# Transposing the query in four pieces, and giving the last unit's products banks of their own with its pieces added and stored one by one

## Chip, cores, metric

One core of one Trainium2 chip. The metric is the device time of one execution, in microseconds (us), as the median of several executions. A ratio in this text is the mean time of one kernel's fast runs over the mean of the other's fast runs of the same rounds, so it is not quite the ratio of the medians that are quoted beside it.

## The reference

```python
def _attn_ref(q, k, v, g_norm):                  # 8 batches x 8 heads x 576 tokens x 64
    kv = np.einsum('bhsd,bhse->bhde', k, v)
    out = np.einsum('bhsd,bhde->bhse', q, kv)
    rms = np.sqrt(np.mean(out * out, axis=-1, keepdims=True) + 1e-06)
    return out / rms * g_norm

def _moe_ref(x, w_a, w_b, w_out):                # 4608 tokens, 512 -> 1536 -> 512
    return (x @ w_a) * (x @ w_b) @ w_out
```

The second takes the first's output, tokens by (heads x 64), as x.

## The kernel before

The program is recorded as nodes (engine, estimated duration, priority, dependencies with latencies, buffers) and put in order by a greedy planner while the kernel is built. **The planner's durations and latencies set only the order of the instructions on each engine; on the chip each instruction waits for semaphores.** An estimate that is too short can therefore not give a wrong result.

```python
class Plan:
    LAT = {"PE": 0.27, "SP": 2.2, "ACT": 0.2, "DVE": 0.18}
    # ... ready(): end of each dependency plus LAT, or plus the latency given with it
    # ... order(): per engine, what can start first; then the lower priority

def load_node(b, prio, dep, xt=None):            # loads of one batch; cut
    def issue():                                 # on GpSimd
        if dep is not None:                      # wait for the q of the batch before
            nc.gpsimd.tensor_copy(gate_t, dep["q"].tile[0:1, 0, 0:1])
        # ... q to DRAM as bf16 (2 DMAs, scr), then k (5 DMAs) and v (2 DMAs) into SBUF
    def transpose():                             # on SP
        nc.sync.dma_start_transpose(
            out=ld["q"].tile[:].rearrange("p a s -> p (a s)"),
            in_=scr[:].rearrange("a s h d -> (a s) (h d)"))
    ld["n"]  = plan.add("POOL", issue_us, prio, issue, [(dep["qn"], 8.0)] ...)
    ld["qn"] = plan.add("SP", 2.5, prio, transpose, [(ld["n"], q_us)], [ld["q"]])

def load_wo(dep):                                # output weights, behind the first such q
    def issue():
        nc.gpsimd.tensor_copy(gate_t, dep["q"].tile[0:1, 0, 0:1])
        # ... two DMAs, wo_t
    return plan.add("POOL", 1.8, 50.0, issue, [(dep["qn"], 8.0)])
```

The output product of the first 512 tokens (`o_std`) has matmuls of 128x512. Its nodes depend on `(wo_n, 5.8)` for the first half and `(wo_n, 10.6)` for the second.

The later output products use seven block products in place of eight (a Winograd form of Strassen's scheme). The last unit, whose stores end the kernel:

```python
# m = 2 row tiles of 128 rows, EH = 256 columns; X, Y, Z, W[i] are PSUM banks
p1 = prod(0, X, a11, b11, True, [], [X])
e1 = ev(0, 0, 0, p1, [ob])                                       # ACT copies X
p2 = prod(1, Y, a12, b21, True, [], [Y])
c11 = comb(1, 0, 0, Y, [p2, e1], [Y])                            # DVE adds
p6 = prod(2, X, sx(s2), t2, False, [e1, n2], (), [s2], 2)        # adds into X
e2 = ev(2, 0, 1, p6)
p5 = prod(3, Z, a21, t1, True, [n1], [Z], (), 1)
e5 = ...                                                         # ACT copies Z to u5
p7 = prod(4, X, sx(s3), t3, False, [e2, n3], (), [s3], 0)        # adds into X
e3 = ev(4, 1, 0, p7)                                             # ACT copies X
c22 = comb(4, 1, 1, X, [p7, e5], [X, u5], u=u5)                  # DVE reads X
p3 = prod(5, Z, sx(s4), b22, False, [e5, n4], (), [s4], 3)       # adds into Z
c12 = comb(5, 0, 1, Z, [p3, e2], [Z])
# ... stores of c11, c22, c12
for i in range(m):
    p4 = prod(6 + 0.1 * i, W[i], a22, t4, True, [n4], [W[i]], subs=slice(i, i + 1))
    c21 = comb(6 + 0.1 * i, 1, 0, W[i], [p4, e3], [W[i]], slice(i, i + 1))
    # ... store of this piece
```

Of the kernel before, what the change touches and what calls it, by code (L numbers as in the profile page):

```python
# [137 lines left out]
def kernel(  # L138
# [11 lines left out]
    nc = tc.nc  # L150
# [258 lines left out]
    def act_us(n, bias=False):  # L409
        return (0.155 if bias else 0.06) + n / 1200  # L410
# [10 lines left out]
        ]  # L421

    T0 = 20.0
    B5, B6, CX, CY = 5, 8, 3, 4
    TB, TURN, AHEAD = 5, 3.0, 8.0
    plan = Plan({"PE": 5.7, "DVE": 3.3, "ACT": 2.7, "SP": 5.0, "POOL": 22.5, "V": 0.0})
# [180 lines left out]
    def late_batch(b, load, win):  # L607
        at = Attn(b)
        w0, w1 = win
        kb, vb, qb = load["k"], load["v"], load["q"]  # L610
        kd = Buf(RKD)
        at.qt = [qb, kd]

        def view(t):
            return t[:, 0 : H * (NCH + 1) * D].rearrange("p (h c d) -> p h c d", h=H, d=D)

        s = Buf(RS5 if b >= TB else RS)

        def kv_mm():
            kv_ps = s.tile[:].rearrange("p (a e) -> p a e", a=NP)  # L620
            for c in range(NCH + 1):
                for p in range(NP):
                    hs = slice(2 * p, 2 * p + 2)
                    nc.tensor.matmul(  # L624
                        kv_ps[:, p, :],
                        lhsT=kb.tile[:, c, hs, :],
                        rhs=view(vb.tile)[:, hs, c, :],
                        start=(c == 0 and p == 0),
                        stop=(c == NCH and p == NP - 1),
                    )  # L630

        n = plan.add(
            "PE", 1.15, w0, kv_mm, [(load["n"], load["kv_us"]), plan.at(w0 - 3)], [s, kd], [kb, vb]
        )

        def kv_out():
            kv_ps = s.tile[:].rearrange("p (a e) -> p a e", a=NP)
            at.kvd = kd.tile
            nc.scalar.copy(at.kvd[0:D, :, 0:D], kv_ps[0:D, :, 0:D])
            nc.scalar.copy(at.kvd[D:, :, D:], kv_ps[D:, :, D:])  # L640
            for p in range(NP):
                at.q[p] = qb.tile[:, p, :]

        m = plan.add("ACT", 0.75, w0, kv_out, [n], (), [s])
        if b >= TB:
            return token_tiles(at, (w0 + 0.12 * (w1 - w0), w1), [m, (load["qn"], 8.0)])
        slices(at, (w0 + 0.12 * (w1 - w0), w1), lambda p: [m, (load["qn"], 8.0)])


    def load_node(b, prio, dep, xt=None):  # L650
        ld = {"k": Buf(RK), "v": Buf(RV), "q": Buf(RQT)}
        scr = scr_pool.tile([NP, S, 2, D], BF16, name="scr", tag="scr")

        def issue():
            if dep is not None:
                nc.gpsimd.tensor_copy(gate_t, dep["q"].tile[0:1, 0, 0:1])
            if xt is not None:
                nc.gpsimd.tensor_copy(gate_t, xcols(NP - 1, (b - 2) * S, 1)[0:1])
            qv = q[b].rearrange("(p hl) s d -> hl s p d", hl=2)
            for hl in range(2):  # L660
                nc.gpsimd.dma_start(  # L661
                    out=scr[:, :, hl, :].rearrange("p s d -> s p d"), in_=qv[hl]
                )
            kt = ld["k"].tile
            ks = k[b, :, 0:SA, :].rearrange("h (sp c) d -> sp h c d", c=NCH)
            for c in range(NCH):
                nc.gpsimd.dma_start(out=kt[:, c], in_=ks[:, :, c, :])  # L667
            nc.gpsimd.dma_start(out=kt[0:SB, NCH], in_=k[b, :, SA:S, :].rearrange("h sp d -> sp h d"))
            for n, src in (("v", v),):
                t = ld[n].tile[:, 0 : H * (NCH + 1) * D].rearrange(  # L670
                    "p (h c d) -> p h c d", h=H, d=D
                )
                nc.gpsimd.dma_start(
                    out=t[:, :, 0:NCH, :],
                    in_=src[b, :, 0:SA, :].rearrange("h (sp c) d -> sp h c d", c=NCH),
                )
                nc.gpsimd.dma_start(
                    out=t[0:SB, :, NCH, :], in_=src[b, :, SA:S, :].rearrange("h sp d -> sp h d")
                )

        def transpose():
            nc.sync.dma_start_transpose(
                out=ld["q"].tile[:].rearrange("p a s -> p (a s)"),
                in_=scr[:].rearrange("a s h d -> (a s) (h d)"),
            )

        issue_us, q_us, ld["kv_us"] = (15.4, 4.3, 13.0) if dep is None else (9.0, 5.0 if b == 3 else 1.8, 16.0 if b == 3 else 13.0)

        ld["n"] = plan.add(
            "POOL", issue_us, prio, issue, ([(dep["qn"], 8.0)] if dep else []) + ([(xt, TURN)] if xt else []), [ld["k"], ld["v"]]  # L690
        )
        ld["qn"] = plan.add(
            "SP", 2.5, prio, transpose, [(ld["n"], q_us)], [ld["q"]]
        )
        return ld

# [1 line left out]

    def load_wo(dep):
        def issue():  # L700
            nc.gpsimd.tensor_copy(gate_t, dep["q"].tile[0:1, 0, 0:1])
            for i in range(2):
                sl = slice(i * FC // 2, (i + 1) * FC // 2)
                nc.gpsimd.dma_start(out=wo_t[:, sl, :], in_=wo_v[:, sl, :])

        return plan.add("POOL", 1.8, 50.0, issue, [(dep["qn"], 8.0)])


    def std_block(win):
# [257 lines left out]
    def o_unit(r0, ab, muls, osum, pr, du, chunks, pieces, m, w, first, second, X, Y, Z, ob, s2, s3, s4, W):  # L967
# [6 lines left out]
        def sx(b):  # L974
            return lambda js: b.tile[:, js, 0:w]
# [52 lines left out]
        def bank(b, subs):  # L1028
            n = subs.stop - subs.start
            return b.tile[:, subs.start * EH : subs.stop * EH].rearrange("p (s e) -> p s e", s=n)  # L1030
# [6 lines left out]
        def ev(off, fi, h, dep, takes=(), frees=()):  # L1037
            return plan.add(
                "ACT", act_us(m * EH), pr + off * du,
                lambda: nc.scalar.copy(o(fi, h), bank(X, every)), [dep], takes, frees,  # L1040
            )

        def comb(off, fi, h, ps, deps, frees=(), subs=every, u=None):
            def add():
                other = u.tile[:, subs] if u else o(fi, h, subs)
                nc.vector.tensor_add(o(fi, h, subs), bank(ps, subs), other)  # L1046

            return plan.add(
                "DVE", dve_us((subs.stop - subs.start) * EH), pr + off * du, add, deps, (), frees
            )  # L1050

        def put(fi, subs, deps, us=0.45, queue="SP", es=slice(0, d_model)):
            q = {"SP": nc.sync, "ACT": nc.scalar}[queue]

            def go():
                for i in range(subs.start, subs.stop):
                    store(r0 + (fi * m + i) * 128, ob.tile[:, fi * m + i], q, es)

            plan.add(queue, us * (subs.stop - subs.start), pr + 7 * du, go, deps, (), [ob])
# [3 lines left out]
        t2, t3, t4 = (so_t[:, i] for i in range(3))  # L1063
        n1, n2, n3, n4 = osum
        if W:
            u5 = Buf(RU)
            p1 = prod(0, X, a11, b11, True, [], [X])
            e1 = ev(0, 0, 0, p1, [ob])
            p2 = prod(1, Y, a12, b21, True, [], [Y])
            c11 = comb(1, 0, 0, Y, [p2, e1], [Y])  # L1070
            p6 = prod(2, X, sx(s2), t2, False, [e1, n2], (), [s2], 2)
            e2 = ev(2, 0, 1, p6)
            p5 = prod(3, Z, a21, t1, True, [n1], [Z], (), 1)
            e5 = plan.add(
                "ACT", act_us(m * EH), pr + 3 * du,
                lambda: nc.scalar.copy(u5.tile[:, every], bank(Z, every)), [p5], [u5],
            )
            p7 = prod(4, X, sx(s3), t3, False, [e2, n3], (), [s3], 0)
            e3 = ev(4, 1, 0, p7)
            c22 = comb(4, 1, 1, X, [p7, e5], [X, u5], u=u5)  # L1080
            p3 = prod(5, Z, sx(s4), b22, False, [e5, n4], (), [s4], 3)
            c12 = comb(5, 0, 1, Z, [p3, e2], [Z])
            e1s, e2s = slice(0, EH), slice(EH, d_model)
            put(0, every, [c11], es=e1s)
            put(1, every, [c22], es=e2s)
            for i in range(m):
                put(0, slice(i, i + 1), [c12], queue=("SP", "ACT")[i], es=e2s)
            for i in range(m):
                subs = slice(i, i + 1)
                p4 = prod(6 + 0.1 * i, W[i], a22, t4, True, [n4], [W[i]], subs=subs)  # L1090
                c21 = comb(6 + 0.1 * i, 1, 0, W[i], [p4, e3], [W[i]], subs)
                put(1, subs, [c21], queue=("ACT", "SP")[i], es=e1s)
            return
        p1 = prod(0, X, a11, b11, True, [(wo_n, 10.6)], [X])
        e1 = ev(0, 0, 0, p1, [ob])
# [45 lines left out]
    for bi in range(1, nb + 1):  # L1141
# [10 lines left out]
        ab, muls = wino_block(bi, (st[bi], st[bi + 1]), wsum)  # L1152
    o_block(
        nb, ab, muls, osum, (st[nb + 1], st[nb + 1] + o_us[nb]), NJ // 2,
        (RO, RY, RY, RS, RQ), NJ // 2,
    )
    order, t = plan.order(), 5.7
    for n in order:
# [34 lines left out]
```

## Time and profile before

| | before |
|---|---|
| time, median (range), 3 runs | 297.67 us (296.86 to 298.25) |
| span of the profiled execution | 294.8 us |
| PE busy | 288.1 us, 98% |
| end of the last matmul | 289.77 us |
| from there to the end of the span ("drain") | 5.00 us |

PE is the tensor engine, DVE the vector engine, ACT the scalar engine, POOL is GpSimd and SP only issues transfers. The trace of each kernel is of one execution, so the single times below (last matmul, drain) are those of one execution. PSUM and SBUF are the two memories on the chip in which the program's tiles lie: X, Y, Z, W and V are in banks of PSUM, inputs, weights and finished sums in SBUF. A line such as "L1008 PE MATMUL bk<-wo_t,abt" gives source line, engine, operation, and output and inputs by the program's names; in brackets stands the idle time of the engine just before and what ended it.

### The profile page before, as it was taken

How to read it: one execution, taken by the hardware profiler on the slowest of the kernel's cores; microseconds unless marked ns; L12 is line 12 of the kernel's file. 1: busy time of each engine (PE TensorE's matmuls, PEld its weight loads, DVE VectorE, ACT ScalarE, POOL GpSimd, SP SyncE). 2: the span in 40 equal slices, each digit the busy share in tenths (PEclk: the TensorE clock that was granted, in tenths of full speed). 3: DMA queues.
4: the chain of work that ended last, by engine and by line, in shares of the span. 5: the costliest groups of instructions: out<-in, count | busy, mean ns of one | idle time of the engine just before them, and what ended most of it. 6: DMA issues, size and time to landing. Idle time of an engine off the chain costs nothing.

```text
span 294.8 us, 6757 instructions
## 1 busy us (share of the span) xinstructions
PE 288.1 (98%) x2646; PEld 238.1 (81%) x2648; DVE 240.2 (81%) x441; ACT 191.7 (65%) x395; POOL 77.1 (26%) x96
## 2 busy tenths in 40 slices
PE   8999999999999999999999999999999999999993
PEld 3645558965888988899988998898988888888882
DVE  5454879893987988789979999979989958788852
ACT  3757667876578677877757866786769546665420
POOL 8945830950092470380001910000000000000000
PEclk9999999999999999999999999999999999999999
DMA  8999999699999999499816999330155001200053
GB/s 181 198 199 200 196 158 166 102 168 183 189 128 171 143 170 173 48 136 210 174 31 149 145 166 167 80 145 21 38 85 165 2 0 43 102 2 0 9 172 107
DMA packets 112643, 36.26 MB, mean 123 GB/s; under 512 B 89060, under 2 KB 108516, under 8 KB 112612
## 3 DMA queue, kind: packets, MB, share of 16 engines
q0 software_dynamic: 77552, 18.44, 65.9%
q1 hardware_dynamic: 34448, 16.70, 26.8%
q10 hardware_dynamic: 612, 0.71, 0.8%
q8 instruction: 20, 0.33, 0.5%
q14 instruction: 11, 0.09, 0.1%
HBM read 37.75 MB, written 14.75 MB: 178 GB/s over the span
## 4 chain that ended last, share of the span: by engine, by line
PE 93%; DVE 4%; issue 1%; ACT 1%; DVEq 0%; ACTq 0%
PE bk L839 47%; PE bk L1008 24%; PE bk L387 7%; PE bk L310 3%; PE bk L943 3%; PE bk L624 2%; PE bk L353 2%; PE bk L367 2%; PE bk L341 1%; PE bk L539 1%; PE bk L325 1%; DVE c L858 1%; DVE so L746 1%; DVE o_sb L1046 1%; DVE T L806 1%
## 5 line engine op out<-in xcount | busy, mean ns | idle before, releaser
L858 DVE TENSOR_TENSOR c<-bk,u 128x512 f16<-128x512 f32 x144 | 96.1, 684 | 19.3 <-PE bk L839 11.8
L420 ACT COPY u<-bk 128x512 f32<-128x512 f32 x144 | 81.4, 591 | 36.5 <-PE bk L839 29.9
L839 PE MATMUL bk<-xp,wa_t 128*128 128x256 f16 x288 | 55.0, 273 | 0.1
L839 PE MATMUL bk<-xp,wb_t 128*128 128x256 f16 x288 | 55.0, 273 | 0.0
L839 PEld LDWEIGHTS <-wa_t 128*128 128x128 f16 x384 | 37.1, 98 | 5.7 <-issue 0.3
L1008 PEld LDWEIGHTS <-abt 128*128 128x128 f16 x384 | 37.5, 98 | 4.7 <-issue 0.3
L839 PEld LDWEIGHTS <-wb_t 128*128 128x128 f16 x384 | 37.6, 98 | 4.4
L1008 PE MATMUL bk<-wo_t,abt 128*128 128x256 f16 x288 | 37.2, 273 | 0.1
L839 PE MATMUL bk<-T,sb 128*128 128x256 f16 x192 | 36.7, 273 | 0.0
L839 PE MATMUL bk<-T,sa 128*128 128x256 f16 x192 | 36.7, 272 | 0.0
L420 ACT CAST c<-bk 128x512 f16<-128x512 f32 x48 | 28.0, 587 | 12.1 <-PE bk L839 11.5
L893 DVE TENSOR_TENSOR abt<-c 128x1024 f16<-128x1024 f16 x48 | 32.7, 684 | 0.9
L839 PEld LDWEIGHTS <-sb 128*128 128x128 f16 x288 | 28.2, 98 | 3.3
L839 PEld LDWEIGHTS <-sa 128*128 128x128 f16 x288 | 27.9, 98 | 3.5
L1008 PEld LDWEIGHTS <-as 128*128 128x128 f16 x288 | 28.1, 98 | 3.3
L1040 ACT COPY o_sb<-bk 128x512 f32<-128x512 f32 x31 | 18.2, 586 | 18.5 <-PE bk L1008 18.0
L376 DVE SCALAR_TENSOR_TENSOR xp<-bk,g_col,rs 128x288 f16<-128x288 f32 x40 | 20.2, 512 | 10.9 <-ACT rs L371 10.9
L1008 PE MATMUL bk<-so,as 128*128 128x256 f16 x192 | 25.2, 273 | 0.0
L371 ACT ACTIVATE rs<-bk,eps_t 128x288 f32<-128x288 f32 x40 | 20.0, 506 | 6.2 <-PE bk L367 6.1
L667 POOL DMA_DIRECT2D k_t<-in_k_dram x24 | 21.2, 899 | 0.8 <-issue 0.5
L661 POOL DMA_DIRECT2D scr<-in_q_dram x12 | 19.6, 1638 | 2.5 <-issue 1.5
L1046 DVE TENSOR_TENSOR o_sb<-bk,o_sb 128x512 f32<-128x512 f32 (+1 forms) x25 | 16.4, 663 | 3.0 <-PE bk L1008 2.3
(107 smaller groups left out, 428.8 us busy)
## 6 DMA issues: line engine op xcount, KB each, us to landing
out_dram<-o_sb SPq DMA_DIRECT2D x20, 256.0 KB, 2.7
scr<-in_q_dram POOLq DMA_DIRECT2D x12, 288.0 KB, 8.0
k_t<-in_k_dram POOLq DMA_DIRECT2D x24, 128.0 KB, 8.2
v_t<-in_v_dram POOLq DMA_DIRECT2D x6, 512.0 KB, 11.0
out_dram<-o_sb SPq DMA_DIRECT2D x18, 128.0 KB, 2.4
wa_t<-in_moe_w_a_dram POOLq DMA_DIRECT2D x6, 256.0 KB, 10.6
wb_t<-in_moe_w_b_dram POOLq DMA_DIRECT2D x6, 256.0 KB, 10.8
wo_t<-in_moe_w_out_dram POOLq DMA_DIRECT2D x2, 768.0 KB, 9.7
```

The source lines that it names most:

```text
L371: nc.scalar.activation(rs, self.s_ps[p, h][:, 0:HF], AF.Abs_reciprocal_sqrt, bias=eps_t)
L376: nc.vector.scalar_tensor_tensor(out=xcols(p, self.b * S + h * HF, HF), in0=self.x_ps[p, h][:, 0:HF], scalar=g_col, in1=self.rs[p, h], op0 ...
L387: nc.tensor.matmul(ps[:, 0:n], lhsT=w[:, kc, fc * 128 : (fc + 1) * 128], rhs=xcols(kc, 0, n), start=(kc == 0), stop=(kc == KC - 1),)
L420: ("ACT", act_us(n), lambda: nc.scalar.copy(*args())),
L661: nc.gpsimd.dma_start(out=scr[:, :, hl, :].rearrange("p s d -> s p d"), in_=qv[hl])
L667: nc.gpsimd.dma_start(out=kt[:, c], in_=ks[:, :, c, :])
L839: nc.tensor.matmul(ps.tile[:, i * n : (i + 1) * n], lhsT=lhs(w, sm)[:, kc, :], rhs=rhs()[:, kc, :], start=start and i == 0 and kc == 0, st ...
L858: lambda: nc.vector.tensor_add(cs(fi, h), full(ps), u.tile),
L893: nc.vector.tensor_mul(t, c[:, :, :, 0], c[:, :, :, 1])
L1008: nc.tensor.matmul(ps.tile[:, sub * EH : (sub + 1) * EH], lhsT=lhs(slice(j, j + 1))[:, 0, sub * 128 : (sub + 1) * 128], rhs=rhs[:, j, :], ...
L1040: lambda: nc.scalar.copy(o(fi, h), bank(X, every)), [dep], takes, frees,
L1046: nc.vector.tensor_add(o(fi, h, subs), bank(ps, subs), other)
```

## The change

Intent: (1) q is transposed in four pieces, one per pair of heads, and the planner is told that SP is held 5.0 instead of 2.5 us, and that q is there 2.5 instead of 8.0 us after that; GpSimd's gates (one-element copies that wait for q) read the last piece. (2) In the last unit, product 7 gets a bank of its own (V) and goes ahead of product 5; products 5 and 3 go by row tile into two banks; ACT's copy of product 7 goes away; c12 is added and stored in two pieces, the last of them alone at the end.

```diff
-            return token_tiles(at, (...), [m, (load["qn"], 8.0)])
+            return token_tiles(at, (...), [m, (load["qn"], 2.5)])
 ...                                                  # the same for slices()
-                nc.gpsimd.tensor_copy(gate_t, dep["q"].tile[0:1, 0, 0:1])
+                nc.gpsimd.tensor_copy(gate_t, dep["q"].tile[0:1, NP - 1, 0:1])
 ...                                                  # the same in load_wo
-            nc.sync.dma_start_transpose(
-                out=ld["q"].tile[:].rearrange("p a s -> p (a s)"),
-                in_=scr[:].rearrange("a s h d -> (a s) (h d)"),
-            )
+            for p in range(NP):
+                nc.sync.dma_start_transpose(
+                    out=ld["q"].tile[:, p, :], in_=scr[p].rearrange("s h d -> s (h d)")
+                )
 ...
-            "POOL", issue_us, prio, issue, ([(dep["qn"], 8.0)] if dep else []) ...
+            "POOL", issue_us, prio, issue, ([(dep["qn"], 2.5)] if dep else []) ...
-            "SP", 2.5, prio, transpose, [(ld["n"], q_us)], [ld["q"]]
+            "SP", 5.0, prio, transpose, [(ld["n"], q_us)], [ld["q"]]
 ...                                                  # load_wo
-        return plan.add("POOL", 1.8, 50.0, issue, [(dep["qn"], 8.0)])
+        return plan.add("POOL", 1.8, 50.0, issue, [(dep["qn"], 2.5)])
 ...                                                  # last unit
-            e2 = ev(2, 0, 1, p6)
-            p5 = prod(3, Z, a21, t1, True, [n1], [Z], (), 1)
-            e5 = ...
-            p7 = prod(4, X, sx(s3), t3, False, [e2, n3], (), [s3], 0)
-            e3 = ev(4, 1, 0, p7)
-            c22 = comb(4, 1, 1, X, [p7, e5], [X, u5], u=u5)
-            p3 = prod(5, Z, sx(s4), b22, False, [e5, n4], (), [s4], 3)
-            c12 = comb(5, 0, 1, Z, [p3, e2], [Z])
+            e2 = ev(2, 0, 1, p6, (), [X])
+            p7 = prod(P7_AT, V, sx(s3), t3, True, [n3], [V], [s3], 0)      # P7_AT = 2.5
+            c2x = ... nc.vector.tensor_add(o(1, 0), bank(V, every), o(0, 1)) ...
+            for i in range(m):
+                p5 = prod(3 + 0.1 * i, Z[i], a21, t1, ..., subs=rows[i])
+                e5.append(... nc.scalar.copy(u5.tile[:, rows[i]], bank(Z[i], rows[i])) ...)
+            c22 = ... nc.vector.tensor_add(o(1, 1), o(1, 0), u5.tile[:, every]) ...
 ...                                                  # p4, c21 by row tile, as before
+            for i in range(m):
+                p3 = prod(6 + 0.1 * i, Z[i], sx(s4), b22, ..., subs=rows[i])
+                c12 = comb(6 + 0.1 * i, 0, 1, Z[i], [p3, e2], [Z[i]], rows[i])
+                put(0, rows[i], [c12], queue=("ACT", "SP")[i], es=e2s)
 ...
-        (RO, RY, RY, RS, RQ), NJ // 2,
+        (RO, RY, RS, RY, RS, RQ, RY), NJ // 2,
```

More of the change, by code (lines that the diff above doesn't have):

```diff
@@ L423 @@
     T0 = 20.0
+    P7_AT = 2.5
     B5, B6, CX, CY = 5, 8, 3, 4
@@ L645, in late_batch @@
         if b >= TB:
-            return token_tiles(at, (w0 + 0.12 * (w1 - w0), w1), [m, (load["qn"], 8.0)])
-        slices(at, (w0 + 0.12 * (w1 - w0), w1), lambda p: [m, (load["qn"], 8.0)])
+            return token_tiles(at, (w0 + 0.12 * (w1 - w0), w1), [m, (load["qn"], 2.5)])
+        slices(at, (w0 + 0.12 * (w1 - w0), w1), lambda p: [m, (load["qn"], 2.5)])
     def load_node(b, prio, dep, xt=None):
@@ L681, in transpose @@
         def transpose():
-            nc.sync.dma_start_transpose(
-                out=ld["q"].tile[:].rearrange("p a s -> p (a s)"),
-                in_=scr[:].rearrange("a s h d -> (a s) (h d)"),
-            )
+            for p in range(NP):
+                nc.sync.dma_start_transpose(
+                    out=ld["q"].tile[:, p, :], in_=scr[p].rearrange("s h d -> s (h d)")
+                )
         issue_us, q_us, ld["kv_us"] = (15.4, 4.3, 13.0) if dep is None else (9.0, 5.0 if b == 3 else 1.8, 16.0 if b == 3 else 13.0)
         ld["n"] = plan.add(
-            "POOL", issue_us, prio, issue, ([(dep["qn"], 8.0)] if dep else []) + ([(xt, TURN)] if xt else []), [ld["k"], ld["v"]]
+            "POOL", issue_us, prio, issue, ([(dep["qn"], 2.5)] if dep else []) + ([(xt, TURN)] if xt else []), [ld["k"], ld["v"]]
         )
         ld["qn"] = plan.add(
-            "SP", 2.5, prio, transpose, [(ld["n"], q_us)], [ld["q"]]
+            "SP", 5.0, prio, transpose, [(ld["n"], q_us)], [ld["q"]]
         )
@@ L700, in issue @@
         def issue():
-            nc.gpsimd.tensor_copy(gate_t, dep["q"].tile[0:1, 0, 0:1])
+            nc.gpsimd.tensor_copy(gate_t, dep["q"].tile[0:1, NP - 1, 0:1])
             for i in range(2):
@@ L1065, in o_unit @@
         if W:
-            u5 = Buf(RU)
+            u5, V, Z = Buf(RU), W[0], [Z, W[1]]
+            W = W[2:]
+            rows = [slice(i, i + 1) for i in range(m)]
             p1 = prod(0, X, a11, b11, True, [], [X])
@@ L1071, in o_unit @@
             p6 = prod(2, X, sx(s2), t2, False, [e1, n2], (), [s2], 2)
-            e2 = ev(2, 0, 1, p6)
-            p5 = prod(3, Z, a21, t1, True, [n1], [Z], (), 1)
-            e5 = plan.add(
-                "ACT", act_us(m * EH), pr + 3 * du,
-                lambda: nc.scalar.copy(u5.tile[:, every], bank(Z, every)), [p5], [u5],
-            )
-            p7 = prod(4, X, sx(s3), t3, False, [e2, n3], (), [s3], 0)
-            e3 = ev(4, 1, 0, p7)
-            c22 = comb(4, 1, 1, X, [p7, e5], [X, u5], u=u5)
-            p3 = prod(5, Z, sx(s4), b22, False, [e5, n4], (), [s4], 3)
-            c12 = comb(5, 0, 1, Z, [p3, e2], [Z])
+            e2 = ev(2, 0, 1, p6, (), [X])
+            p7 = prod(P7_AT, V, sx(s3), t3, True, [n3], [V], [s3], 0)
+            c2x = plan.add(
+                "DVE", dve_us(m * EH), pr + 4 * du,
+                lambda: nc.vector.tensor_add(o(1, 0), bank(V, every), o(0, 1)), [p7, e2], (), [V],
+            )
+            e5 = []
+            for i in range(m):
+                p5 = prod(3 + 0.1 * i, Z[i], a21, t1, True, [n1], [Z[i]], (), 1, subs=rows[i])
+                e5.append(
+                    plan.add(
+                        "ACT", act_us(EH), pr + 3 * du,
+                        lambda i=i: nc.scalar.copy(u5.tile[:, rows[i]], bank(Z[i], rows[i])),
+                        [p5], [] if i else [u5],
+                    )
+                )
+            c22 = plan.add(
+                "DVE", dve_us(m * EH), pr + 4.2 * du,
+                lambda: nc.vector.tensor_add(o(1, 1), o(1, 0), u5.tile[:, every]), [c2x] + e5, (), [u5],
+            )
             e1s, e2s = slice(0, EH), slice(EH, d_model)
@@ L1086, in o_unit @@
             for i in range(m):
-                put(0, slice(i, i + 1), [c12], queue=("SP", "ACT")[i], es=e2s)
+                p4 = prod(5 + 0.1 * i, W[i], a22, t4, True, [n4], [W[i]], subs=rows[i])
+                c21 = comb(5 + 0.1 * i, 1, 0, W[i], [p4, c22], [W[i]], rows[i])
+                put(1, rows[i], [c21], queue=("ACT", "SP")[i], es=e1s)
             for i in range(m):
-                subs = slice(i, i + 1)
-                p4 = prod(6 + 0.1 * i, W[i], a22, t4, True, [n4], [W[i]], subs=subs)
-                c21 = comb(6 + 0.1 * i, 1, 0, W[i], [p4, e3], [W[i]], subs)
-                put(1, subs, [c21], queue=("ACT", "SP")[i], es=e1s)
+                p3 = prod(6 + 0.1 * i, Z[i], sx(s4), b22, False, [e5[i], n4], (), [s4], 3, subs=rows[i])
+                c12 = comb(6 + 0.1 * i, 0, 1, Z[i], [p3, e2], [Z[i]], rows[i])
+                put(0, rows[i], [c12], queue=("ACT", "SP")[i], es=e2s)
             return
```

## The prediction

> **What bounds the kernel now.** I read the page's busy times and slices first, then the waits of the tensor engine, the busy times by stretch, and at the end the timeline and transfers of the last 7 us.
>
> The page of the kernel before, busy times, slices, chain:
>
> ```profile
> span 294.8 us, 6757 instructions
> PE 288.1 (98%) x2646; PEld 238.1 (81%) x2648; DVE 240.2 (81%) x441; ACT 191.7 (65%) x395; POOL 77.1 (26%) x96
> ...
> PE   8999999999999999999999999999999999999993
> ...
> PE 93%; DVE 4%; issue 1%; ACT 1%; DVEq 0%; ACTq 0%
> ```
>
> Only the first and the last slice of PE are not full, and the chain that ended last is 93% PE. PE's own waits over the whole span are two, both in the first microseconds:
>
> ```profile
> PE bk L310 <- DVE eps_t L274: 1.2, 1, 1.2
> PE bk L310 <- issue: 0.2, 1, 0.2
> ```
>
> Since "busy" is modelled from overlapping matmuls, I also went through the spacing of the matmul starts. A 256-column matmul follows the one before by 0.109 us; after 43 us only three intervals are longer than the work explains, by some 0.27 us near 80.7, 0.07 near 193.0 and 0.27 near 226.3, and none has a data wait beside it (0.6 us in all). So from 24 us to the last matmul PE is limited by its own work. By stretch (us; PE, PEld, DVE, ACT, POOL busy with counts; clock; DMA; GB/s):
>
> ```profile
> 268.00:280.40 12.40, 12.40 (x116) 11.13 (x114) 10.82 (x21) 5.08 (x9) 0.00 (x0) 1.00 0.05 17
> 280.40:289.80 9.40, 9.37 (x86) 8.15 (x84) 5.02 (x10) 2.34 (x4) 0.00 (x0) 1.00 0.38 120
> 289.80:294.80 5.00, 0.00 (x0) 0.00 (x0) 1.26 (x4) 0.00 (x0) 0.00 (x0) 0.86 0.48 157
> ```
>
> The last unit's 84 matmuls (7 products x 12) fill 280.4 to 289.8. Then 5.0 us follow without a matmul: this drain is the only place after the start where time is not PE work. Its timeline (start, length, engine):
>
> ```profile
> 288.29 1.47 PE L1008 MATMUL bk<-wo_t,as 128*128 128x256 f16 x12
> 288.49 0.59 ACT L1040 COPY o_sb<-bk 128x512 f32<-128x512 f32 x1 [1.16 <-PE bk L1008]
> 289.11 0.69 DVE L1046 TENSOR_TENSOR o_sb<-bk,u 128x512 f32<-128x512 f32 x1 [3.80 <-ACT o_sb L1040]
> 289.72 1.34 DVE L1046 TENSOR_TENSOR o_sb<-bk,o_sb 128x256 f32<-128x256 f32 x3
> 289.83 1.80 SPq L911 DMA_DIRECT2D out_dram<-o_sb  x4
> 290.21 1.29 ACTq L911 DMA_DIRECT2D out_dram<-o_sb  x2
> ```
>
> Product 7 ends at 288.45. ACT copies the shared bank X until 289.08, and only then may DVE begin c22 from the same bank; the two halves of c21 follow, and c12, whose matmuls ended at 289.77 (0.27 after the last start, 289.50), comes last, 290.38 to 291.06 (the third of the group at 289.72). So DVE starts c12 0.6 us late and does it in one 512-column piece. All six stores are issued between 289.83 and 291.24, and their data run back to back (stretch 288 to 295 in 40 slices of 0.175 us):
>
> ```profile
> DMA  0000000000000006979999999999800000000000
> GB/s 0 0 0 0 0 0 0 0 0 0 0 0 0 0 0 217 328 240 339 345 345 334 322 369 328 334 351 339 281 24 0 0 0 0 0 0 0 0 0 0
> ```
>
> Six stores of 128 KB are 0.79 MB; at some 335 GB/s that is 2.35 us, which is what the full slices show (290.6 to 293.2). SP sees the last landing at 293.55; checks and barriers take to 294.76.
>
> **What the Trainium skill says.** "PSUM — Partial Sum Buffer", section "PSUM bank collisions raise a hardware error": two engines may not touch one bank and quadrant at the same time, two readers included, so ACT and DVE reads of one bank have to be ordered. The trace agrees: c22 starts 0.03 us after the ACT copy of the same bank. "VectorE: DVE Perf Modes", "The perf-mode tier table": a float32 tensor_tensor runs at 1x whether it reads SBUF or PSUM. That matters for the new c22, which reads SBUF alone; no such operation is in this trace, so I take the 0.69 us of the PSUM one. "DMA: Bandwidth & Descriptors", "Anatomy of one DMA": a transfer has a fixed cost of about 2.0 us, mostly the receipt of the last byte. The lone store at 285.34 landed after 1.7 us, the six of the end after 2.0 to 2.3, so the trace agrees roughly, and shows that queueing adds 0.3 to 0.6.
>
> **The change part by part.**
>
> First part, the q pieces. One DMA transpose of all of q becomes four, one per head pair. Existing rows give both forms: the whole one (qT), and pieces of the same size in another place (xp), with SP's own time for one instruction (min/median/max ns) and time to landing:
>
> ```profile
> L682 SPq DMA_TRANSPOSE qT<-scr x6: 5981/6398/6860, 42.0 to 171.8; - x6
> L594 SPq DMA_TRANSPOSE xp<-xs x12: 1152/1254/2024, 153.4 to 219.4; - x12
> ...
> qT<-scr SPq DMA_TRANSPOSE x6, 10.3
> xp<-xs SPq DMA_TRANSPOSE x12, 2.7
> ```
>
> Before: q is there 10.3 us after the issue. After: the fourth piece is issued 3 x 1.30 = 3.9 us after the first (their starts lie 1.3 apart) and lands 2.7 later, 6.6 us in all; SP is held 5.2 instead of 6.4 us. So q is ready some 3.7 us earlier, six times, and the next load can follow earlier. Who waits for q:
>
> ```profile
> POOL gate_t L656 <- DMA qT<-scr: 46.4, 4, 13.1
> POOL gate_t L701 <- DMA qT<-scr: 11.0, 1, 11.0
> ```
>
> It is POOL, which only issues loads; no PE wait for q is listed. So the 3.7 us is worth 0 in the time, beyond at most the 0.6 us of unexplained intervals. The schedule's assumption (5.0 + 2.5 us after the start) is 0.9 above my 6.6, so PE should not be sent to a q that is not there.
>
> Second part, the last unit. PE work: the same 84 matmuls, split by row tile in three products; 0. Removed: the ACT copy after product 7 (0.59) and the DVE wait for it. Product 7 gets a bank V, starts fresh instead of adding to X, and moves ahead of product 5; the sum with X's value moves to DVE (c2x, 0.69). c22 becomes an SBUF add (estimated 0.69). DVE work on the unit after product 7 goes from c22, c21 x2, c12 to c2x, c22, c21 x2, c12 x2: one 512-column add more, but off the path, since now products 5, 4 and 3 (3 x 1.31 = 3.9 us of PE) follow product 7.
>
> Schedule backwards from a last matmul that still ends at 289.77: product 3's second row tile 289.12 to 289.77 (6 x 0.109), its first 288.46 to 289.12, product 4 before 288.46, product 5 before 287.15. ACT's two copies of product 5 are then done by about 287.6, c22 by 288.3, the c21 pieces by about 289.1 (2 x 0.33 to 0.42), c12's first piece by 289.55, so DVE is free when the last piece comes. It starts 0.04 after the matmul's end (product 7 to ACT was 288.45 to 288.49) and takes the 0.415 us of a 256-column add: 289.81 to 290.22. Before: 291.06. **Gain on the path: 0.84 us.**
>
> Stores: those of c22 and of c21 now go out from about 288.3, c12's first at 289.6, so when the last is issued at 290.26 (0.03 after the add) there is little queue. Before, the last was issued at 291.24 (0.18 after its add, behind another on SP) and seen landed at 293.55, 2.3 later. After: 290.26 + 1.7 to 2.2 = 291.96 to 292.46, middle 292.2. Gain at the landing 1.1 to 1.6, middle **1.35**, of which 0.84 is DVE, 0.15 the issue, the rest the shorter queue. The closing checks cost 0.06 us each and their order may shift, +-0.2.
>
> Sum: 0 (q) - 1.35 (end) + 0.15 that I allow for a reordered schedule = -1.2 us. 297.67 - 1.2 = **296.5 us**.
>
> **The rivals.** (a) Store bandwidth stays the bound: the same 0.79 MB has to leave, and if the schedule puts c22 and c21 late, all six stores again come together. For it: the full 2.35 us now. Against: two of them need only products 5 to 7. Then the gain is 0.84 at most, 296.8. (b) DVE is the bound: it has one more add, and if product 5's copies come late, c22, c21 and c12 queue behind it and the last add ends as late as before: 297.5. Against: DVE has only 5.0 busy of 9.4 us there. (c) Earlier loads reorder the compile-time schedule, so that PE meets a bank or a load that is not free, or needs seven banks in the last unit where there were five: 0.3 to 2 us lost, 297 to 299. Against: products 1, 5 and half of 4 have banks outside the two that Y, V and W share, enough to fill while the last multiply (ends 282.36) is awaited. (d) The q pieces win more: removes the odd intervals, 0.5 more, 295.9. Little speaks for it.
>
> **Range and chances.** The drain is 5.0 us, of which about 2.5 us (receipt, barriers) can't go; so the gain can't reach 2% (5.95 us). A loss of that size would need stalls in a row that nothing here hints at. The three runs of before spread 296.86 to 298.25, so I take 295.5 to 297.4 for 8 in 10. Faster by over 2%: 0.01; within: 0.98; slower: 0.01.
>
> **What would show it.** PE busy near 288 and no new PE wait; the gate's waits for q shorter and the q pieces at about 1.25 us each; no ACT copy after product 7; a last DVE piece of 128x256 about 0.04 us after the last matmul, 0.42 long; last matmul to end of span about 3.7 instead of 5.0 us; stores spread from 288 on. I am wrong if the last matmul moves by over 0.5 us, if DVE is still working off c22 or c21 at 289.8, or if the DMA row is full until over 292.5.

## The result

The changed kernel took 297.26 us (median of 6 runs, 296.59 to 297.75), the kernel before 297.49 us in the same 6 rounds; ratio 0.9991, 95% interval 0.997 to 1.0012. That is the same time. The predicted gain of 1.2 us is not there.

Two parts of the profile have to be read separately. PE's waits over the whole span, kernel after:

```profile
PE bk L944 <- DMA wo_t<-in_moe_w_out_dram: 1.9, 2, 1.2
PE bk L310 <- DVE eps_t L274: 1.2, 1, 1.2
```

The first line is new: PE waited twice for the output weights. Where it stood, in PE's timeline of the kernel after:

```profile
58.88 0.38 PE L840 MATMUL bk<-xp,sb 128*128 128x256 f16 x2
60.51 0.59 PE L944 MATMUL bk<-wo_t,abt 128*128 128x512 f16 x2 [1.25 <-DMA wo_t<-in_moe_w_out_dram]
...
63.69 0.38 PE L840 MATMUL bk<-xp,sb 128*128 128x256 f16 x2
64.76 1.45 PE L944 MATMUL bk<-wo_t,abt 128*128 128x512 f16 x6 [0.69 <-DMA wo_t<-in_moe_w_out_dram]
```

By the starts of the matmuls the two intervals are 1.52 and 0.96 us, where 0.11 is normal: 1.41 + 0.85 = 2.26 us lost. The interval of 0.27 us too long near 80.7 of the kernel before is gone; the last matmul ends at 291.78 instead of 289.77, so 2.01 later. The chain of work that ended last now runs through those weights (kernel after, its pieces in order of time: start, length, what):

```profile
46.52 5.44 DMA qT<-scr
51.96 0.05 issue
52.01 0.64 POOL gate_t L702
52.65 0.76 POOL wo_t L705
53.41 11.31 DMA wo_t<-in_moe_w_out_dram
...
64.76 1.45 PE bk L944 x6
```

q's last piece lands at 51.96 and opens GpSimd's gate; the weights are issued; their second half lands 11.3 us later and PE has been waiting for it. In the kernel before the gate opened at the same time (its copy starts at 51.94, after at 52.01). So the pieces brought the whole of q not a moment earlier. What moved is the first reader of the weights: in the order as built it is matmul 517 instead of 534 (in the trace of before, which has two matmul records fewer, the 532nd).

The end did become shorter. Its timeline, kernel after (groups of the kernel before are in the prediction):

```profile
288.82 0.69 DVE L1079 TENSOR_TENSOR o_sb<-bk,o_sb 128x512 f32<-128x512 f32 x1 [1.49 <-PE bk L1009]
...
289.66 0.69 DVE L1093 TENSOR_TENSOR o_sb<-o_sb,u 128x512 f32<-128x512 f32 x1
...
290.31 1.47 PE L1009 MATMUL bk<-wo_t,as 128*128 128x256 f16 x12
290.46 1.13 DVE L1047 TENSOR_TENSOR o_sb<-bk,o_sb 128x256 f32<-128x256 f32 x3
...
291.82 0.42 DVE L1047 TENSOR_TENSOR o_sb<-bk,o_sb 128x256 f32<-128x256 f32 x1 [0.23 <-PE bk L1009]
```

c2x (L1079), c22 (L1093), the two pieces of c21 and the first of c12 (the group of 3 at 290.46) are done while PE still multiplies; DVE is idle for 0.23 us before the last 256-column add. c22, which reads SBUF alone, took 0.69 us like c2x, which reads PSUM, as the prediction assumed. The transfers from 288 to 295 us, kernel after (40 slices of 0.175 us, as in the prediction):

```profile
DMA  0895992000000000005977999999999930000000
GB/s 0 275 339 164 310 322 88 0 0 0 0 0 0 0 0 0 0 0 176 334 234 252 339 328 357 316 351 351 328 345 340 339 106 0 0 0 0 0 0 0
```

The last six stores still move their data back to back, but they begin before the last matmul ends: the slices are full until 293.6, 1.8 us after the last matmul's end, where before it was 3.3. Following the last store through single instructions of the two traces gives this sum (us):

| from the last matmul's end to | before | after | gain |
|---|---|---|---|
| start of the last add | 0.62 | 0.04 | 0.58 |
| its end | 0.68 | 0.43 | 0.26 |
| issue of the last store | 0.18 | 0.06 | 0.11 |
| its landing, as SP sees it | 2.31 | 1.83 | 0.47 |
| end of the span (further checks, barriers) | 1.22 | 1.08 | 0.13 |
| **drain** | **5.00** | **3.44** | **1.55** |

So 1.55 us were gained at the end, and the last matmul came 2.01 us later: 2.26 lost near 59 to 65 us, less the 0.27 that is gone. The profiled pair nets +0.46 us, the medians -0.23; the difference lies in the runs' scatter (the profiled run of before, 296.94, was one of its quicker ones).

### The profile page after: what moved, and what is told of

Its sections match the earlier page's. It is cut to its first block, busy times and chain, and to the rows that moved or that the text cites. A ratio compares the mean times of both kernels' runs of the same rounds, so it can differ in the third digit from the quotient of the medians.

```text
span 295.2 us, 6794 instructions
## 1 busy us (share of the span) xinstructions
PE 288.4 (98%) x2648; PEld 238.0 (81%) x2648; DVE 241.6 (82%) x443; ACT 191.0 (65%) x395; POOL 77.9 (26%) x96
## 4 chain that ended last, share of the span: by engine, by line
PE 76%; DMA 16%; POOL 4%; SPq 1%; issue 1%; DVE 1%; ACT 0%; ACTq 0%; POOLq 0%
PE bk L840 44%; PE bk L1009 25%; DMA scr<-in_q_dram 4%; DMA wo_t<-in_moe_w_out_dram 4%; DMA wb_t<-in_moe_w_b_dram 4%; DMA wa_t<-in_moe_w_a_dram 3%; PE bk L944 3%; PE bk L625 2%; DMA qT<-scr 2%; SPq L684 1%; POOL as L242 1%; PE bk L540 1%; PE bk L367 1%; PE bk L353 1%; POOL so L242 1%
## 5 line engine op out<-in xcount | busy, mean ns | idle before, releaser
L1041 ACT COPY o_sb<-bk 128x512 f32<-128x512 f32 x30 | 17.6, 586 | 16.4 <-PE bk L1009 16.0
```

Of the source, the lines that this page charges most:

```text
L1041: lambda: nc.scalar.copy(o(fi, h), bank(X, every)), [dep], takes, frees,
```

## The experiments

**The end alone.** The changed kernel with part (1) taken back:

```diff
-            for p in range(NP):
-                nc.sync.dma_start_transpose(out=ld["q"].tile[:, p, :], ...)
+            nc.sync.dma_start_transpose(out=ld["q"].tile[:].rearrange(...), ...)
 # SP 5.0 -> 2.5, (qn, 2.5) -> (qn, 8.0) everywhere
```

> Only the last unit is changed; q is one transpose again, with the old latencies in the schedule. Theory (the last unit saves some 1.6 us of the drain, and the q part costs about as much as PE waits for the output weights near 59 to 65 us): last matmul near 289.8 us as in the kernel before, drain 3.4 us in place of 5.0, time 1.5 us under before, ratio 0.995, no PE wait for the output weights. Rival (the end only looks shorter because the last matmul comes later, the new bank plan itself delays PE): ratio 0.999 or above, last matmul near 291.

Measured: 295.68 us against 297.09, ratio 0.9952 (0.994 to 0.9964). Last matmul 290.18, drain 3.55, no PE wait for the output weights. The last matmul is 0.4 us later than in the kernel before, but this delay is not the new bank plan's: counted by the columns of the matmuls done, PE is already 0.4 us behind at 22.7 us, long before the last unit. The end is a real gain.

**The q part alone.** The kernel before with part (1), pieces and planner latencies.

> Only the q pieces and their new latencies in the schedule; the last unit as before. Theory: two PE waits of together about 2.2 us for the output weights, the last matmul 2 us later, drain 5.0 us as before, time 2 us over before, ratio 1.007. Rival (the q part is neutral): ratio 1.000.

Measured: 298.64 us against 297.09, ratio 1.0055 (1.0042 to 1.0068); drain 4.88, last matmul 291.35. Of its PE waits, the one that is new:

```profile
PE bk L943 <- DMA wo_t<-in_moe_w_out_dram: 1.7, 2, 1.4
```

The loss is real, by intervals 1.60 + 0.40 = 2.0 us; it shows as 1.55 in the medians, somewhat under the 2 expected, as again the 0.27 near 80.7 is not there.

**The latencies alone.** The kernel before, with q in one transpose:

```diff
-            "SP", 2.5, prio, transpose, ...
+            "SP", 5.0, prio, transpose, ...
 # (qn, 8.0) -> (qn, 2.5) everywhere; nothing else
```

> The kernel before with one transpose of all of q, but with the new latencies in the schedule (5.0 + 2.5 us instead of 2.5 + 8.0). Theory (the cost is the schedule's belief that q, and so the load behind it, comes 3 us earlier, not the pieces): the same two PE waits as with the pieces, 2 us over before, ratio 1.007. Rival (four pieces crowd the queue and delay the output weights' load): no wait, ratio 1.000.

Measured: 298.21 us against 297.09, ratio 1.005 (1.0032 to 1.0068). No transfer was changed, and the wait is there:

```profile
60.06 0.59 PE L943 MATMUL bk<-wo_t,abt 128*128 128x512 f16 x2 [0.56 <-DMA wo_t<-in_moe_w_out_dram]
...
64.28 1.02 PE L943 MATMUL bk<-wo_t,abt 128*128 128x512 f16 x4 [0.66 <-DMA wo_t<-in_moe_w_out_dram]
```

The intervals are 0.72 and 0.83 us too long, 1.55 together. So the estimate in the planner is enough to lose the time; the rival, that the pieces crowd the queue, is not needed.

**True latencies, pieces kept.** The changed kernel with `(qn, 2.5)` -> `(qn, 5.5)` everywhere.

> The changed kernel with the pieces kept, but the schedule told 5.0 + 5.5 us for q, the sum of before and about what the pieces were measured to take. Theory: no PE wait for the output weights, last matmul near 289.8, drain 3.4 us, ratio 0.995 as with the last unit alone. Rival (the pieces cost time themselves): ratio 0.999 or above.

Measured: 295.28 us against 297.09, ratio 0.994 (0.9928 to 0.9952); last matmul 290.26, drain 3.44, no wait for the weights. As the theory has it, but for the last matmul, which is 0.5 later than expected; 0.4 of that is again there at 22.7 us.

**One latency put right, at the load.** Only `load_wo` gets 5.5.

```diff
-        return plan.add("POOL", 1.8, 50.0, issue, [(dep["qn"], 2.5)])
+        return plan.add("POOL", 1.8, 50.0, issue, [(dep["qn"], 5.5)])
```

> The changed kernel, with one latency of the schedule put right: the output weights' load waits for q + 5.5 us instead of q + 2.5; everything else that reads q still believes 2.5. Theory (the early order of the first output products is the whole loss): no PE wait for the output weights, last matmul near 290.2, ratio 0.994 to 0.996, as with all latencies put right. Rival (other readers of q are also sent too early): PE waits elsewhere, ratio 0.998 or above.

Measured: 308.9 us against 296.85, ratio 1.0408. Far from both expectations. GpSimd's timeline of this run shows why:

```profile
52.00 0.75 POOL L657 COPY gate_t<-qT 1x1 bf16<-1x1 bf16 x1 [10.89 <-DMA qT<-scr]
52.69 3.25 POOL L662 DMA_DIRECT2D scr<-in_q_dram  x2
...
61.65 0.18 POOL L702 COPY gate_t<-qT 1x1 bf16<-1x1 bf16 x1
61.77 1.66 POOL L705 DMA_DIRECT2D wo_t<-in_moe_w_out_dram  x2
```

The later estimate made the planner put the whole next batch's load ahead of the weights in GpSimd's queue. They were issued at 61.8 instead of 52.6, and PE waited 8.7 us for them. Most of the rest of the 12 us are some 2 us of smaller waits between 61 and 67 us, and matmuls at a lower granted clock just behind the wait (0.60 from 76 to 82 us; those of 512 columns start 0.43 us apart, against 0.21 in the kernel after). The edit answered another question than the one it was made for; it shows how much hangs on the order in which the loads are issued.

**The same at the readers.** All latencies of q as in the changed kernel; the readers of the weights get 3.0 us more, which leaves GpSimd's order as it is:

```diff
-                    [(wo_n, 5.8 if f0 + OP <= FC // 2 else 10.6), n1] + ...
+                    [(wo_n, 8.8 if f0 + OP <= FC // 2 else 13.6), n1] + ...
 # and the two other (wo_n, 10.6) -> 13.6
```

> The changed kernel with all its optimistic q latencies, but each reader of the output weights told 3.0 us more (8.8 and 13.6 instead of 5.8 and 10.6), so that the order in which GpSimd issues the loads stays and only the readers move; by the built order the first output product then stands at the same place among the matmuls as in the kernel before. Theory (the readers' place is the whole loss): no PE wait for the output weights above 0.3 us, last matmul near 290.2, ratio 0.994 to 0.996. Rival (other readers of q are also too early): waits elsewhere, ratio 0.998 or above.

Measured: 295.33 us against 297.17, ratio 0.9941 (0.992 to 0.9961); last matmul 289.58, drain 3.46, no wait for the weights. So the place of these readers is the whole loss; the other readers of q are not sent too early.

**The bank alone.** The kernel with true latencies, product 7 in its bank V and moved ahead, but products 5 and 3 whole in one bank, c12 one add of 512 columns.

```diff
-            for i in range(m):
-                p5 = prod(3 + 0.1 * i, Z[i], ..., subs=rows[i]); e5.append(...)
+            p5 = prod(3, Z, a21, t1, True, [n1], [Z], (), 1); e5 = [...]
-            for i in range(m):
-                p3 = prod(6 + 0.1 * i, Z[i], ..., subs=rows[i]); c12 = comb(..., rows[i])
+            p3 = prod(6, Z, ...); c12 = comb(6, 0, 1, Z, [p3, e2], [Z])
```

> Last unit with product 7 in a bank of its own and moved ahead, but products 5 and 3 whole in one bank and c12 in one 512-column add; q as in the kernel with the latencies put right. Theory (both parts count): the last add takes 0.69 instead of 0.42 us and both of its stores come after it, so the drain is 3.39 + 0.27 + some 0.2 = 3.8 to 3.9 us, ratio 0.9955 to 0.996. Rival (all of the gain is the row split): drain near 5.0, ratio 0.999. Rival (all of it is the bank): drain 3.4, ratio 0.994.

Measured: 296.66 us against 296.85, ratio 1.000 (0.9981 to 1.0018); last matmul 290.29, drain 4.11. The drain lies between the two rivals, as the theory has it, but is 0.2 to 0.3 longer than its number. Against the 3.44 of the full end, 0.27 is the longer add (0.69 against 0.42), 0.38 the landing (2.21 us after the issue instead of 1.83: both of c12's stores are issued together, at 291.04 and 291.05), and 0.05 the checks after it (less 0.03 at the issue). I had put all but the add at 0.2. The time missed the expectation: a ratio of 1.000 is nearer the first rival's 0.999 than 0.9955. The six runs lie far apart (296.09 to 297.93), and in the profiled one PE is 0.5 us behind the kernel before by 22.8 us; that the bank alone gains is read from the drain, and the times do not show it.

**The row split alone.** Products 5 and 3 by row tile, c12 in two pieces, but product 7 adds into bank X and ACT copies it.

```diff
-            p7 = prod(P7_AT, V, sx(s3), t3, True, [n3], [V], [s3], 0); c2x = ...
+            p7 = prod(4, X, sx(s3), t3, False, [e2, n3], (), [s3], 0)
+            e3 = ev(4, 1, 0, p7); c22 = comb(4, 1, 1, X, [p7] + e5, [X, u5], u=u5)
```

> Last unit with products 5 and 3 by row tile in two banks and c12 in two pieces stored at once, but product 7 still adds into the bank of products 1 and 6, is copied by ACT and sits just ahead of product 3. Theory (ACT and DVE taking turns on that bank make DVE late): ACT copy, then c22, two pieces of c21, two of c12 queue on DVE until some 1.3 to 1.5 us after the last matmul, as before; drain 4.6 to 5.0, ratio 0.998 to 1.000. Rival (the row split alone gives it): drain near 3.5, ratio 0.995.

Measured: 297.04 us against 296.85, ratio 1.0012 (0.9993 to 1.0032); last matmul 290.94, drain 4.88. Its timeline:

```profile
289.47 1.47 PE L1009 MATMUL bk<-wo_t,as 128*128 128x256 f16 x12
289.67 0.58 ACT L1041 COPY o_sb<-bk 128x512 f32<-128x512 f32 x1 [1.54 <-PE bk L1009]
290.28 0.69 DVE L1047 TENSOR_TENSOR o_sb<-bk,u 128x512 f32<-128x512 f32 x1 [3.80 <-ACT o_sb L1041]
290.89 1.41 DVE L1047 TENSOR_TENSOR o_sb<-bk,o_sb 128x256 f32<-128x256 f32 x4
```

DVE waits for ACT's copy of the bank as before and works off its queue until 292.30, 1.36 us after the last matmul. The row split alone gives 0.12 us of drain, about what two closing checks fewer behind the last landing are worth (see below); it gives 0.67 us (4.11 - 3.44) once product 7 is out of the way. (PE was also 0.7 us behind the kernel before by 23 us and met a short wait for the output weights here, an interval 0.34 us too long at 61.5, so the drain and not the time is the measure. The same order with true latencies met none in two other runs; it has little slack.)

**The pieces without the loads beside them.** The changed kernel without the k and v loads of the batch with index 4. Its output is wrong, which doesn't matter for the time.

```diff
             for c in range(NCH):
-                nc.gpsimd.dma_start(out=kt[:, c], in_=ks[:, :, c, :])
+                if b != 4:
+                    nc.gpsimd.dma_start(out=kt[:, c], in_=ks[:, :, c, :])
+            if b == 4:
+                return                                    # no rest of k, no v
```

> The changed kernel without the k and v loads of the batch with index 4, on purpose wrong in its result; the third set of four q pieces then has the DMA engines nearly to itself. Theory (a piece lands late because it shares the DMA engines with the k and v loads): those four pieces land 2.5 to 3 us after their issue, like those of xp, and the last some 6.6 us after the first issue, the other sets still 5 to 8 us. Rival (pieces of this source are slow in themselves): 5 to 8 us for those four too.

Measured, for that batch's four pieces (transfers issued from 89.2 to 99.2 us of this run):

```profile
qT<-scr SPq DMA_TRANSPOSE x4, 2.8
```

The same four pieces in the kernel after (89.7 to 99.7 us):

```profile
v_t<-in_v_dram POOLq DMA_DIRECT2D x1, 512.0 KB, 8.6
qT<-scr SPq DMA_TRANSPOSE x4, 7.3
```

The last column is the median time to landing in us. Without the k and v loads the pieces land like those of xp, and the last of them 6.6 us after the first issue, the very sum of the prediction. So the theory holds: what makes them late is the traffic beside them, not their source.

**The pieces with true latencies, old end.**

> The kernel before with the four q pieces and the latency of 5.0 + 5.5 us in the schedule; the last unit as before. Theory (with a true latency the pieces neither gain nor cost, because only GpSimd waits for q): ratio 0.999 to 1.001, drain 5.0. Rival (the pieces give the 0.4 us by which the kernel with pieces and true latencies beat the one with the end alone): ratio 0.9985 or below.

The edit is the q part alone with `(qn, 5.5)` in place of `(qn, 2.5)`. Measured: 296.60 us against 297.17, ratio 0.9979 (0.9962 to 0.9996). That misses "0.999 to 1.001": a gain of some 0.6 us in the medians, just clear of zero. No PE wait tells of it (the last matmul is at 290.01, and the intervals that are 0.27 us too long are there as before, at 80.8 and 226.5). The drain is 4.87 instead of 5.00: SP's closing checks follow in a fixed order, 0.06 us each, and in this trace four of them follow the last landing, where before six did; from the landing to the end it takes 1.08 instead of 1.22 us. Nearly the same separates the kernel with pieces and true latencies (1.09) from the end alone (1.20). Where the rest of the 0.6 comes from is open.

**A try at a better version.** Pieces, q latency 5.5, and readers of the weights 1.0 us later.

> An attempt at a better version: pieces, q latency 5.5, and 1.0 us more for the readers of the output weights, so that the first of them has some slack (by the built order six matmuls later). If the remaining slack of the kernel with true latencies is what limits it: ratio 0.993; if not, the same 0.994 as without; if the moved order meets another wait: over 0.995.

Measured: 297.28 us against 297.17, ratio 0.9998 (0.9981 to 1.0014). The third case came true: the moved order meets other small waits of PE,

```profile
PE bk L840 <- DVE o_sb L1047: 0.3, 1, 0.3
PE bk L387 <- DMA wb_t<-in_moe_w_b_dram: 0.3, 1, 0.3
PE bk L944 <- ACT o_sb L960: 0.2, 1, 0.2
```

and its last store landed 2.80 us after its issue, not 1.83; why it did is open.

**A version that beats both kernels** is thus at hand in two forms: the new end with pieces and q latencies of 5.5 (295.28 us, 0.994), or with the readers of the weights told 3.0 us more (295.33 us, 0.9941). They are not told apart, and they were not run beside the changed kernel: the comparison is by ratios to the kernel before, against 0.9991.

## Why the prediction was right or wrong

The measured 297.26 us lies in the range of 295.5 to 297.4, and "within 2%" was right. The mechanism behind the 296.5 was half right. That the range held was partly luck: its upper end takes in only the mildest part of rival (c) (297 to 299), and a loss that the sum did not hold nearly cancelled the gain. By the prediction's own sign ("I am wrong if the last matmul moves by over 0.5 us") it was wrong: the last matmul moved by 2.01.

- *"PE is limited by its own work; the drain is the only place after the start."* Right: the end alone gave 0.9952.
- *"Gain on the path: 0.84 us."* Right: 0.58 + 0.26 = 0.84 between the last matmul and the last add's end. c22, c21 and the first piece of c12 were done 1.43, 0.57 and 0.19 us ahead of the last matmul's end; my backward count had 1.47, 0.67 and 0.22.
- *"Middle 1.35"* at the landing: nearly right, 1.42. Issue 0.11 (0.15 predicted), landing 0.47 (0.36); the checks gave 0.13 more (0 +- 0.2), 1.55 in all. The stores did spread, the first of them going out 1.40 us ahead of the last matmul's end (1.47 in my count), and the last landed after 1.83 us, inside my 1.7 to 2.2. (The "lone" store at 285.34 was not quite alone: another was issued 0.38 us later.)
- **The step that failed: "The fourth piece is issued 3.9 us after the first and lands 2.7 later, 6.6 us in all."** The 2.7 came from xp's pieces, whose stretches had a DMA share of 0.40 to 0.46. q's pieces run beside the k and v loads, at a share near 1.6 (the share adds up the times of all packets over 16 engines, so it can pass 1). There a piece lands after 7.5 us (median), and the last of a set lands 9.8 to 12.3 us after the first issue, where the single transpose took 9.9 to 11.9. Taking the loads away brings back 2.8. SP was held 6.4 to 7.2 us per set, not 5.2, and the gates' waits for q hardly shrank (46.4 + 11.0 us before, 44.9 + 10.9 after).
- **So this failed with it: "The schedule's assumption (5.0 + 2.5 us after the start) is 0.9 above my 6.6, so PE should not be sent to a q that is not there."** It lies 2.3 to 4.8 us below the true 9.8 to 12.3. And what PE was sent to early was not q but the output weights, whose load GpSimd holds back until q is there. I had read "POOL, which only issues loads; no PE wait for q is listed" as a licence to count 0. In the plan those loads have readers too.
- *"+0.15 that I allow for a reordered schedule"* is the mis-sized term: 2.01 us later at the last matmul. Rival (c) gave 0.3 to 2 us for such a loss; its cause was named as a bank or a load that is not free, and it was the load. The seven banks cost no wait that any profile shows.
- Rivals (a) and (b) do not hold: DVE is idle 0.23 us before the last add, and the last store sees little queue (1.83 us to its landing, against 1.72 for the first of the six). Rival (d) had the pieces remove the odd intervals; with true latencies they gain 0.6 us while those intervals stay, so its cause is not shown, and of the gain 0.13 is the closing checks and the rest open.

## What to carry to other kernels

A latency written into a planner is a statement about one place in the program: measure it there, with the traffic that runs beside it; here a row of the same operation elsewhere was off by a factor of 2.8 (2.7 against 7.5 us). A wait on an engine that "only issues loads" is not free of consequence when an order is planned from it; follow it to the first reader of each load. And when two engines must read one PSUM bank at the end of a kernel, try giving one of the products another bank first: here smaller last pieces paid only then (0.67 us of drain with it, 0.12 without).

## What the Trainium skill lacked or had wrong

- "VectorE: DVE Perf Modes", section "The three transpose paths", gives the crossbar transpose by DMA as 1309 ns for 128x128 bf16. Here a piece of 576x128 held SP for 1.32 us in the median (1.13 to 2.94) and landed 2.5 to 2.9 us after its issue with the k and v loads away, and after 5.4 to 8.4 us beside the k and v loads. That page has no figure for the second case, which decided this one.
- "DMA: Bandwidth & Descriptors", section "DMA Transpose (X-bar)", says nothing of splitting one transpose. Here four pieces landed as a whole no earlier than the one transpose (last piece 9.8 to 12.3 us after the first issue, against 9.9 to 11.9).
- The same page, "Anatomy of one DMA", puts the fixed cost of a transfer issued by GpSimd at about 2.0 us; the page has no such fit for stores from SP or ACT. Here a 128 KB store from SP landed 1.72 to 1.74 us after its issue with none just ahead of it, and the last one of the shorter drain after 1.83, transfer included.
- None of the pages used here tells of the checks with which the program ends: each took 0.06 us on SP, in a fixed order, so two fewer of them behind the last landing (four in place of six) were worth some 0.12 us.
